# Retention and mixture of experts on one core: expert jobs of full slots dealt out between the chunks of the retention

## The chip, the cores and the metric

The kernel runs on one NeuronCore of a Trainium2 chip. The core has five engines that take their own instructions in order: PE (TensorE, matrix products), ACT (ScalarE), DVE (VectorE), POOL (GpSimd) and SP (SyncE, which here issues most of the DMA transfers). The weight loads of PE are listed apart as PEld. Times are microseconds of device time for one execution of the whole program; the metric is the median of several runs. The profile is of one further execution.

## The reference

The reference does two things, one after the other. The first is a retention: for each of 4 sequences and 8 heads, a 64 x 64 state decays by a factor per head and takes in k and v of each of 768 tokens; q times the state is the output.

```python
for t in range(S):                      # q, k, v: (4, 8, 768, 64)
    state = gamma * state + k[t] v[t]^T
    y[t] = scale * q[t] @ state
x = y.transpose(0, 2, 1, 3).reshape(3072, 512)
```

The second sends each of the 3072 rows of x to one of 8 experts:

```python
logits = x @ w_gate + modality_bias[modality_id]    # (3072, 8)
e = argmax(logits); gate = softmax(logits)[e]
out = gate * (relu(x @ w1[e]) @ w2[e])              # w1: 512 x 1024, w2: 1024 x 512
```

Which rows go to which expert is known only once the retention has run. With the inputs of the reference, 1567 rows go to expert 0, 1502 to expert 3 and 3 to expert 5; the others get none. After 6, 9, 15, 18, 21 and 24 chunks of 128 rows the counts of experts 0 and 3 are 399 and 368, 578 and 573, 979 and 940, 1187 and 1114, 1386 and 1299, 1567 and 1502.

## The kernel before

**Retention.** The 3072 tokens are worked in 24 chunks of 128, six for each sequence. `chunk(n)` (line 693) loads k and v (`load_kv`, for chunk n+2) and k and q (`load_kq`, for chunk n+3), 512 KB each, on SP's queue; POOL scales v by the decay (`decay_v`, tile vd); PE adds to the state (`state`, st), makes the scores of the next chunk (`scores`, sc), which DVE masks (tile a), turns the chunk before into token rows and logits (`tokens_out`, x; ACT copies to xs, SP stores to `x_dram`), and makes the chunk's own output from the state and from the scores (`heads_out`, y at lines 187 and 193; DVE scales it into yT). A chunk has thus a first half, st and sc, and a second half, x and y. The matrix products of this stage are in full fp32.

**Routing.** After each three chunks (a group), `route_a`, `route_b` and `scatter` (lines 239 to 303) find each token's expert and its position in the expert's list, on DVE with a few small matmuls (rk), and POOL writes token number and gate weight into a table in DRAM, `tbl`, in three indirect transfers.

**Slots and units.** The table has 96 candidates, twelve slots of 256 rows for each expert. A slot of 256 rows is one long job, a unit of 128 rows a short one. After six groups, `early_a` and `early_b` pick the two largest slots; after the last group, `final_a` and `final_b` rank all slots and write the list of the other ten slots and of what is left, in units. A register loop at the end of the kernel (`For_i` from 2 to the number of units) does units beyond the first two; with these inputs there are two units, so it runs zero times.

**Jobs.** `jobs` (line 644) is eleven slots, two units and the last slot. For each job, SP reads expert and row from the list into registers, loads the row numbers (`ids`), POOL gathers the rows from `x_dram` (xg), SP loads the expert's weights into `raw` tiles, four of 512 KB for each of the two layers, unless the expert is that of the job before (`cond=(e != old)`). ACT and DVE cut each raw piece into a high and a low part (`split_weights`, lines 462 and 464), so that three fp32r products (`PAIRS`) stand for one of fp32. PE transposes the gathered rows (`xp`), runs the first layer (line 522 for a slot, 96 matmuls of 256 columns in eight groups; 542 for a unit) and the second (line 570, 48 matmuls of 512 columns for a slot, in two halves of the rows). ACT scales the result by the gate weight and POOL scatters it to the output (line 580).

**Order.** The loop over the 24 chunks stands first. Small things are hung into it by `at(n, where, ...)`: the routing of group g into chunks 3g+4 and 3g+5; for group 5, the early list into chunks 18 and 19, registers and gathers of the first two jobs into chunk 20, the weights of the first job into chunk 21. Then `run_jobs` (line 621) goes through the jobs: a job's successor gets its registers, rows and first-layer weights at the start of the job, its first-layer cut and second-layer load between the layers, its second-layer cut at the end. The last routing and the final list are hung into the first job. This order of the program is a priority, not the last word: a planner that works with its own estimate of each instruction's time fixes each engine's order when the program is built, and takes an instruction early where its engine would stand idle and buffers are free. On the chip that order is kept, each engine strictly in order.

## Time and profile before

| | |
|---|---|
| median of 3 runs | 476.25 us (474.18 to 478.75) |
| profiled execution, its own time | 478.72 us |
| its span, first to last instruction | 476.3 us |
| mean granted PE clock | 0.951 |
| PE busy | 428.3 us, 3647 matmuls |
| DVE, ACT, POOL busy | 265.9, 209.5, 115.5 us |
| moved by q1 (SP) / by q0 (POOL) | 54.32 MB / 13.14 MB |

The page shows busy times over the whole span, and since the kernel has two stages with different limits, the views by stretch and by instruction say more than the totals. In these views, idle time before an instruction stands in brackets with what ended it. The granted clock is that of PE, 1.00 being full. The names are those of the program, with `_s` for slots and `_u` for units; `sc`, `st`, `x` and `y` belong to the retention, `xp`, `h` and `o` to the jobs.

### The profile page before, as it was taken

The page shows a single profiled execution, that of the slowest core. Times are in us where ns is not written, and L with a number is a line of the kernel's source. Part 1 is how long each engine was busy: PE and PEld are TensorE (multiplying, and loading weights), DVE is VectorE, ACT ScalarE, POOL GpSimd, SP SyncE. Part 2 cuts the span into 40 slices and gives each one's busy share as a digit, 9 for nine tenths or more (in the row PEclk, how much of TensorE's full clock was granted, in tenths as well). Part 3 has the DMA queues.
Part 4 walks back from the last instruction along what each step waited for, and adds up shares of the span by engine and source line. Part 5 has one row for each costly group of instructions (what it writes and reads, how often), then busy time and mean ns, then how long its engine had stood idle before and what let it go on. Part 6 is the DMA issues. An engine that isn't in the chain of part 4 may idle for free.

```text
span 476.3 us, 10044 instructions
## 1 busy us (share of the span) xinstructions
PE 428.3 (90%) x3647; PEld 383.6 (81%) x3647; DVE 265.9 (56%) x532; ACT 209.5 (44%) x363; POOL 115.5 (24%) x109
## 2 busy tenths in 40 slices
PE   4968989696929999999999999999999999999990
PEld 4857878585817989898989898989898989888980
DVE  2544644375508967475757574746565656588500
ACT  1211211121216546464646565656565656589400
POOL 3214343342433133231303012213030202121100
PEclk9999997898875999999999999999999999999996
DMA  8988979969658202201113562111120447577000
GB/s 290 329 272 273 247 216 270 226 190 225 208 173 335 46 23 68 67 28 64 33 58 103 170 194 67 29 61 54 38 64 26 143 153 243 187 233 308 2 24 16
DMA packets 36242, 68.53 MB, mean 144 GB/s; under 512 B 8159, under 2 KB 20703, under 8 KB 36192
## 3 DMA queue, kind: packets, MB, share of 16 engines
q1 hardware_dynamic: 30976, 54.32, 38.4%
q0 software_dynamic: 4928, 13.14, 8.1%
q8 instruction: 29, 0.48, 0.5%
q10 hardware_dynamic: 288, 0.42, 0.2%
q14 instruction: 21, 0.17, 0.2%
HBM read 92.55 MB, written 13.59 MB: 223 GB/s over the span
## 4 chain that ended last, share of the span: by engine, by line
PE 57%; issue 8%; DMA 3%; DVE 1%; POOL 1%; ACT 1%; SPq 1%; POOLq 0%; ACTq 0%
PE h_s L522 26%; PE o_s L570 26%; PE xp_s L508 2%; DMA raw<-in_w_dram 2%; DMA tbl<-rows,pos 1%; PE o_u L570 1%; PE uh_u L542 1%; POOL out_dram L580 1%; DVE lo_s L464 1%; PE x L208 0%; SPq L454 0%; PE y L187 0%; ACT hs_u L548 0%; ACT hi_u L462 0%; SPq L483 0%
## 5 line engine op out<-in xcount | busy, mean ns | idle before, releaser
L464 DVE TENSOR_TENSOR lo_s<-raw,hi_s 128x1024 fp32r<-128x1024 f32 x96 | 117.2, 1223 | 81.4 <-ACT hi_s L462 80.0
L462 ACT CAST hi_s<-raw 128x1024 fp32r<-128x1024 f32 x96 | 100.2, 1044 | 29.6 <-PE o_s L570 14.6
L522 PE MATMUL h_s<-xTh,hi_s 128*128 128x256 f32 x384 | 108.5, 283 | 0.0
L522 PE MATMUL h_s<-xTh,lo_s 128*128 128x256 f32 x384 | 108.3, 283 | 0.0
L522 PE MATMUL h_s<-xTl,hi_s 128*128 128x256 f32 x384 | 107.9, 283 | 0.1
L570 PE MATMUL o_s<-hi_s,hTh 128*128 128x512 f32 x192 | 76.2, 397 | 0.0
L570 PE MATMUL o_s<-lo_s,hTh 128*128 128x512 f32 x192 | 75.6, 394 | 0.0
L570 PE MATMUL o_s<-hi_s,hTl 128*128 128x512 f32 x192 | 75.5, 393 | 0.0
L522 PEld LDWEIGHTS h_s<-xTh,lo_s 128*128 128x128 f32 x384 | 73.6, 192 | 0.5
L522 PEld LDWEIGHTS h_s<-xTh,hi_s 128*128 128x128 f32 x384 | 73.6, 192 | 0.5
L522 PEld LDWEIGHTS h_s<-xTl,hi_s 128*128 128x128 f32 x384 | 73.2, 192 | 0.3 <-DVE xTl L478 0.3
L580 POOL DMA_INDIRECT out_dram<-o_s,ids_s x24 | 27.0, 1126 | 153.3 <-ACT o_s L579 148.5
L472 ACT ACTIVATE hTh<-h_s 128x256 fp32r<-128x256 f32 x96 | 36.8, 384 | 60.2 <-PE h_s L522 56.2
L473 DVE SCALAR_TENSOR_TENSOR hTl<-h_s,hTh 128x256 fp32r<-128x256 f32 x96 | 40.2, 420 | 27.4 <-ACT hTh L472 27.3
L212 ACT COPY xs<-x 128x272 f32<-128x272 f32 x48 | 17.4, 386 | 74.7 <-DMA x_dram<-xs 31.8
L208 PE MATMUL x<-wgt,yT 128*128 128x136 f32 x192 | 33.4, 325 | 16.7 <-DVE yT L200 16.3
L171 DVE TENSOR_TENSOR a<-sc,cst 128x512 f32<-128x512 f32 x48 | 31.0, 684 | 27.5 <-PE sc L166 23.4
L489 POOL DMA_INDIRECT xg_s<-x_dram,ids_s x24 | 29.6, 1233 | 66.6 <-PE h_s L522 29.0
L652 POOL TENSOR_TENSOR vd<-kv,cst 128x512 f32<-128x512 f32 x24 | 25.4, 1057 | 81.0 <-DMA kv<-in_qkv_dram 64.1
L208 PEld LDWEIGHTS x<-wgt,yT 128*128 128x128 f32 x192 | 28.2, 219 | 19.4 <-ACT s L233 11.0
L570 PEld LDWEIGHTS o_s<-lo_s,hTh 128*128 128x128 f32 x192 | 36.0, 188 | 8.1
L570 PEld LDWEIGHTS o_s<-hi_s,hTl 128*128 128x128 f32 x192 | 36.1, 188 | 7.8
(160 smaller groups left out, 515.3 us busy)
## 6 DMA issues: line engine op xcount, KB each, us to landing
raw<-in_w_dram SPq DMA_DIRECT2D x112, 512.0 KB
kv<-in_qkv_dram SPq DMA_DIRECT2D x24, 512.0 KB
kq<-in_qkv_dram SPq DMA_DIRECT2D x23, 512.0 KB
x_dram<-xs SPq DMA_DIRECT2D x24, 256.0 KB
dcq<-in_decq_dram SPq DMA_DIRECT2D x6, 256.0 KB
tbl<-rows,pos POOLq DMA_INDIRECT x24, 6.5
xg_s<-x_dram,ids_s POOLq DMA_INDIRECT x24, 3.9
out_dram<-o_s,ids_s POOLq DMA_INDIRECT x24, 2.8
```

Source lines behind the costliest of these rows:

```text
L171: evac[n] = nc.vector.tensor_tensor(a[:, j], pe[j].rearrange("p (h t) -> p h t", t=P), mask.unsqueeze(1).to_broadcast([P, NG, P]), op=ALU. ...
L208: nc.tensor.matmul(px[:, g], yT[:, 2 * u + g], wgt[:, 2 * u + g], start=(g == 0), stop=(g == 1), skip_group_check=True,)
L212: nc.scalar.copy(xs[:, 2 * u : 2 * u + 2], px)
L462: nc.scalar.copy(hi, raw)
L464: nc.vector.tensor_tensor(lo, raw, hi.bitcast(F32), op=ALU.subtract)
L472: nc.scalar.activation(hi, src, AF.Relu)
L473: nc.vector.scalar_tensor_tensor(lo, src, 0.0, hi.bitcast(F32), op0=ALU.max, op1=ALU.subtract)
L489: nc.gpsimd.indirect_dma_start(out=t[:, :], out_offset=None, in_=x_dram[:avail, :], in_offset=bass.IndirectOffsetOnAxis(ap=ids[:, hh, 0:1] ...
L522: nc.tensor.matmul(ph, w1c[f // 2][wi][:, o : o + P], xT[kc // 2][a][:, kc % 2, :], start=(n == 0), stop=(n == 3 * KC - 1),)
L570: nc.tensor.matmul(po, hT[f][a][:, hh * P : (hh + 1) * P], w2c[f // 2][wi][:, (f % 2) * DM : (f % 2 + 1) * DM], start=(n == 0), stop=(n == ...
L580: ins = nc.gpsimd.indirect_dma_start(out=out[:, :], out_offset=bass.IndirectOffsetOnAxis(ap=ids[:, hh, 0:1], axis=0), in_=o[:, :], in_offs ...
L652: nc.gpsimd.tensor_tensor(vds[n], vv, dec[:, n % NCH].unsqueeze(2).to_broadcast([P, H, D]), op=ALU.mult)
```

## The change

The retention is now a generator that yields after each half of a chunk, and a job is one that yields after each eighth of the first layer and after each quarter of each half of the second: 16 steps for a slot, 8 for a unit. Up to the first half of chunk 10 (`DENSE`) the retention runs alone. From there on jobs run, and after every fourth step of a job comes one half of a chunk, four halves in a slot.

For this, full slots are listed on the way: after groups 1, 2, 4, 5 and 6 (`EVENTS`), each list names two slots that are full by then and not named before. A slot that an early list does not find is replaced by an empty one (candidate 96, whose rows of the table are never written). Ties are broken by the candidate's number, upward or downward (+1 or -1), so that the last expert of a list is the first of the next. The final list has two slots and the units; the order at the end is slot, unit, slot, unit. There is room for 40 units in place of 16.

Routing is dealt out by `tick`: one entry of `todo` after each half chunk or job step. The ranking keeps one column where it had a matrix and a column, and spreads the keys with a product of ones and a diagonal. `split_weights` is now `cut`, piece by piece: the second-layer pieces are cut in the job's own first steps, the first-layer pieces of the next job in the second half of the job. A job's successor starts at its fourth step: registers, ids, gather, then first-layer weights; second-layer weights follow at the ninth step, the transposes at the thirteenth. The first job gets its registers, gather and both layers of weights at the end of chunk 7. The decay tiles `dcq` have memory of their own, vd has two buffers where it had three, and four gather buffers are set to zero in chunk 2.

```diff
-EARLY_GRP = 6
-NEARLY = 2
+
+
+EVENTS = {1: -1, 2: 1, 4: -1, 5: 1, 6: -1}
+NEV = 2
+NFIN = NSLOT - NEV * len(EVENTS)
 NTAIL = 2
-NUNIT = 16
+NUNIT = 40
+DENSE = 10
...
-    dcq = []
-    for i, tag in enumerate(("hi22", "lo22", "dcq2")):
-        dcq.append(me.tile([P, 2, NG, P], F32, tag=tag, name=f"dcq{i}"))
+    dcq = [cp.tile([P, 2, NG, P], F32, name=f"dcq{i}") for i in range(NCH // 2)]
...
+    def ranks(t, counts, which):
+        crep = passing("crep", [P, NE, SPE], BF16)
+        nc.vector.tensor_copy(crep, counts.unsqueeze(2).to_broadcast([P, NE, SPE]))
+        pc = bank(f"pc{t}")
+        nc.tensor.matmul(
+            pc[:NCAND, 0:1], crep.rearrange("p e i -> p (e i)"), ones[:, 0:1],
+            start=True, stop=True,
+        )
+        size = passing("size", [NCAND, 1])
+        nc.vector.tensor_scalar(size, pc[:NCAND, 0:1], off_c, 0.0, op0=ALU.subtract, op1=ALU.max)
+        nc.vector.tensor_scalar(
+            size, size, float(SLOT), mid["keep"], op0=ALU.min, op1=ALU.mult
+        )
+        key = passing("key", [NCAND, 1])
+        nc.vector.scalar_tensor_tensor(
+            key, size, float(P), id_c, op0=ALU.mult, op1=ALU.add if which > 0 else ALU.subtract
+        )
+        dg = passing("dg", [NCAND, NCAND])
+        nc.vector.tensor_scalar(dg, ident[:NCAND, :NCAND], key, None, op0=ALU.mult)
+        mid["rk"] = (t, size, key, dg)
+
+    def ranked():
+        t, size, key, dg = mid.pop("rk")
+        pk = bank(f"pk{t}")
+        nc.tensor.matmul(pk[:NCAND, :NCAND], lc["onef"], dg, start=True, stop=True)
+        gt = passing("gt", [NCAND, NCAND])
+        nc.vector.tensor_scalar(gt, pk[:NCAND, :NCAND], key, None, op0=ALU.is_gt)
+        rank = passing("rank", [NCAND, 1])
+        nc.vector.tensor_reduce(rank, gt, axis=AX.X, op=ALU.add)
+        return size, rank
+
+    def early(g):
+        size, rank = ranked()
+        full = passing("full", [NCAND, 1])
+        nc.vector.tensor_scalar(full, size, float(SLOT), None, op0=ALU.is_ge)
+        ohs = passing("ohs", [NCAND, NEV], BF16)
+        nc.vector.tensor_scalar(
+            ohs, lc["ord_r"][:, :NEV], rank, full, op0=ALU.is_equal, op1=ALU.mult
+        )
+        vals = lc["vals"]
+        pt = bank(f"pt{g}")
+        for i in range(2):
+            nc.tensor.matmul(
+                pt[:1, i * NEV : (i + 1) * NEV], vals[:, i : i + 1], ohs, start=True, stop=True
+            )
+        tk = passing("tk", [NCAND, 1])
+        nc.vector.tensor_reduce(tk, ohs, axis=AX.X, op=ALU.add)
+        keep = passing("keep2", [NCAND, 1])
+        nc.vector.tensor_tensor(keep, mid["keep"], tk, op=ALU.subtract)
+        mid["keep"] = keep
+        lst = lists[g] = small(f"lst{g}", [1, 2 * NEV], I32)
+        nc.vector.tensor_tensor(lst, pt[:1, : 2 * NEV], lc["base_e"], op=ALU.add)
+
...
-    def split_weights(m, tag):
-        chunks = []
-        for i, raw in enumerate(raws[m]):
-            hi = me.tile([P, QW], F32R, tag=f"hi{m}{i}", name=f"hi{m}{i}_{tag}")
-            nc.scalar.copy(hi, raw)
-            lo = me.tile([P, QW], F32R, tag=f"lo{m}{i}", name=f"lo{m}{i}_{tag}")
-            nc.vector.tensor_tensor(lo, raw, hi.bitcast(F32), op=ALU.subtract)
-            chunks.append((hi, lo))
-        return chunks
+    def cut(s, m, i):
+        hi = me.tile([P, QW], F32R, tag=f"hi{m}{i}", name=f"hi{m}{i}_{s['tag']}")
+        nc.scalar.copy(hi, raws[m][i])
+        lo = me.tile([P, QW], F32R, tag=f"lo{m}{i}", name=f"lo{m}{i}_{s['tag']}")
+        nc.vector.tensor_tensor(lo, raws[m][i], hi.bitcast(F32), op=ALU.subtract)
+        s.setdefault(f"w{m}", []).append((hi, lo))
 
...
+    def both(s):
+        yield from first_slot(s) if s["nh"] == 2 else first_unit(s)
+        yield from second(s)
+
+
+
+    def run_job(k):
+        cur = state_of[k]
+        long = cur["nh"] == 2
+        last = k + 1 == len(jobs)
+        nxt = None
+        for t, _ in enumerate(both(cur)):
+            if not long or t % 2 == 0 and t < 8:
+                i = t // 2 if long else t
+                if i < 4:
+                    cut(cur, 2, i)
+            if not last:
+                if t == (3 if long else 0):
+                    nxt = state_of[k + 1] = start_job(jobs[k + 1])
+                    raw(nxt, 1, cur)
+                if t == (8 if long else 4):
+                    raw(nxt, 2, cur)
+                if long and t in (9, 11, 13, 15):
+                    cut(nxt, 1, (t - 9) // 2)
+                if not long and t >= 4:
+                    cut(nxt, 1, t - 4)
+                if t == (12 if long else 6):
+                    flip_x(nxt)
+            yield
+
+
+    jobs = [("e", g, i) for g in EVENTS for i in range(NEV)]
+    for i in range(max(NFIN, NTAIL)):
+        jobs += [("s", 0, i)] * (i < NFIN) + [("u", 0, i)] * (i < NTAIL)
     state_of = {}
...
-        vds[n] = wk.tile([P, H, D], F32, tag="vd", name=f"vd_{n}", bufs=3)
+        vds[n] = wk.tile([P, H, D], F32, tag="vd", name=f"vd_{n}", bufs=2)
...
+    todo = []
+
+    def tick():
+        if todo:
+            todo.pop(0)()
+
+    def route(gr):
+        def b():
+            route_b(gr)
+            if gr in EVENTS or gr == NGRP - 1:
+                ranks(gr, cnt[gr + 1], EVENTS.get(gr, 1))
+
+        def c():
+            scatter(gr)
+            if gr in EVENTS:
+                early(gr)
+            elif gr == NGRP - 1:
+                final_a()
+
+        todo.append(lambda: [route_a(gr, i) for i in range(3)])
+        todo.extend([b, c])
+        if gr == NGRP - 1:
+            todo.append(final_b)
+
+    def retention():
+        prev = st = s = None
+        cur = scores(0)
+        for n in range(NN):
+            c = n % NCH
+            a, qv = cur
+            if n + 2 < NN:
+                load_kv(n + 2)
+            if n + 3 < NN:
+                load_kq(n + 3)
+            if 0 < n < NCH:
+                nc.sync.dma_start(dcq[n // 2][:, n % 2], decq[:, n])
+            if n == 1:
+                with tc.issue_after(evac[0].ins):
+                    setup()
+            if n == 2:
+                list_consts()
+
+                for i in range(4):
+                    z = me.tile([P, DM], F32, tag=f"xg{i % 2}", name=f"xgz{i}", bufs=2)
+                    nc.gpsimd.memset(z, 0.0)
+            if n + 1 < NN:
+                decay_v(n + 1)
+            vd = vds.pop(n)
+            nxt = None
+            if c + 1 < NCH:
+                if c == 0:
+                    st = bank(f"st_{n}")[:, : NG * D].rearrange("p (g e) -> p g e", g=NG)
+                nxt = state(n, st, vd)
+            if n + 1 < NN:
+                cur = scores(n + 1)
+            yield n
+            if prev is not None:
+                tokens_out(*prev)
+                if n % GRP == 0:
+                    route(n // GRP - 1)
+            yT = heads_out(n, a, vd, qv, s)
+            prev = (n, yT)
+            s = nxt
+            yield n
+        tokens_out(*prev)
+        route(NGRP - 1)
+        yield NN
+
...
-    cur = scores(0)
-    for n in range(NN):
-        chunk(n)
-    job = state_of[jobs[0]]
+    ret = retention()
+    for n in ret:
+        tick()
+        if 0 not in state_of and min(EVENTS) in lists:
+            job = state_of[0] = start_job(jobs[0])
+            raw(job, 1)
+            raw(job, 2)
+        if n == DENSE:
+            break
     flip_x(job)
-    tokens_out(*prev)
-    cut(job, 1)
-    cut(job, 2)
-
-    for i in range(3):
-        route_a(NGRP - 1, i)
-
-    def finish_a():
-        route_b(NGRP - 1)
-        scatter(NGRP - 1)
-        final_a(cnt[NGRP], lists["taken"])
-
-    run_jobs(jobs, state_of, {5: finish_a}, {0: final_b})
+    for i in range(4):
+        cut(job, 1, i)
+    for k in range(len(jobs)):
+        for t, _ in enumerate(run_job(k)):
+            tick()
+            if t % 4 == 1:
+                next(ret, None)
+    assert next(ret, None) is None and not todo
 
```

More of the change, by code (lines that the diff above doesn't have):

```diff
@@ L393, in final_a @@
[L393 to L400 removed]
+        onef = small("onef", [NCAND, NCAND])
+        nc.gpsimd.memset(onef, 1.0)
@@ L644 @@
-    jobs = [("s", i) for i in range(NSLOT - 1)]
-    jobs += [("u", i) for i in range(NTAIL)] + [("s", NSLOT - 1)]
+    def both(s):
[23 more added lines that the diff above has]
+                    flip_x(nxt)
+            yield
@@ L769 @@
         flip_x(s)
-        cut(s, 1)
-        cut(s, 2)
-        hT = first_unit("dyn", s["xT"], s["w1"], {})
-        second("dyn", 1, hT, s["w2"], s["ids"], {})
+        for m in (1, 2):
+            for i in range(4):
+                cut(s, m, i)
+        for _ in both(s):
+            pass
 def _layout(inputs):
```

328 lines of the change are left out of this document (98 added, 230 removed).

## Prediction

> **What bounds the kernel now.** I read the page first, then the busy times in four stretches, then the chain that ended last, then PE's own timeline.
>
> ```profile
> span 476.3 us, 10044 instructions
> ...
> PE 428.3 (90%) x3647; PEld 383.6 (81%) x3647; DVE 265.9 (56%) x532; ACT 209.5 (44%) x363; POOL 115.5 (24%) x109
> ```
>
> ```profile
> 0.00:62.00 62.00, 49.82 (x723) 43.34 (x723) 30.80 (x104) 12.31 (x32) 18.50 (x26) 0.97 0.93 283
> 62.00:155.60 93.60, 70.63 (x927) 60.83 (x926) 45.85 (x143) 22.83 (x53) 33.92 (x33) 0.82 0.82 227
> 155.60:464.50 308.90, 307.78 (x2002) 279.48 (x2000) 189.30 (x287) 173.69 (x279) 62.09 (x51) 1.00 0.30 96
> 464.50:476.30 11.80, 0.04 (x1) 0.00 (x0) 0.00 (x0) 0.69 (x1) 0.98 (x1) 0.61 0.04 16
> ```
>
> The columns of a stretch are its length, the busy time of PE, weight load, DVE, ACT and POOL, the granted clock, the DMA share and GB/s. PE is the engine to follow, but its 90% is an average over two different things. From 155.6 to 464.5 us the expert jobs run: PE is busy for 307.78 of 308.90 us at clock 1.00, so there is nothing to gain inside. From 62.0 to 155.6 us, the retention from chunk 10 to the end, PE is busy for 70.63 of 93.60 us, and at clock 0.82. The stretch before 62.0 stays as it is. The chain of waits shows how the jobs follow each other (start, length, what):
>
> ```profile
> 180.72 11.50 PE h_s L522 x96
> ...
> 251.09 11.50 PE h_s L522 x96
> 262.59 0.87 PE xp_s L508 x8
> 263.46 11.07 PE o_s L570 x48
> 274.53 11.50 PE h_s L522 x96
> ```
>
> A full slot costs 274.53 - 251.09 = 23.44 us and PE passes to the next one without a gap. How dense a chunk of the retention can be is on PE's timeline (start, length, line, shape; in brackets the idle time before and what ended it):
>
> ```profile
> 50.10 1.09 PE L193 MATMUL y<-a,vd 128*64 128x128 f32 x16
> ...
> 60.87 1.16 PE L166 MATMUL sc<-kq 64*128 64x128 f32 x16
> ...
> 78.98 1.16 PE L166 MATMUL sc<-kq 64*128 64x128 f32 x16
> 80.08 1.19 PE L208 MATMUL x<-wgt,yT 128*128 128x136 f32 x8
> 81.20 0.67 PE L187 MATMUL y<-kq,s 64*64 64x128 f32 x16
> 81.80 1.09 PE L193 MATMUL y<-a,vd 128*64 128x128 f32 x16
> 82.72 0.64 PE L228 MATMUL st<-vd,kv 128*64 128x64 f32 x16
> 83.28 1.16 PE L166 MATMUL sc<-kq 64*128 64x128 f32 x16
> ...
> 143.69 2.15 PE L208 MATMUL x<-wgt,yT 128*128 128x136 f32 x8 [10.30 <-DVE yT L200]
> ...
> 155.63 0.37 PE L522 MATMUL h_s<-xTh,hi_s 128*128 128x256 f32 x1
> ```
>
> From one sc to the next, 78.98 to 83.28, a chunk takes 4.30 us when nothing holds PE up: sc 1.10, x 1.12, y from the state 0.60, y from the scores 0.92, st 0.56 (differences of the starts). The group at 60.87 is the scores that chunk 10 makes for chunk 11. Between the two halves of the picture lies a pause: at 143.69 PE had waited 10.30 us, and its eight x matmuls then took 2.15 us where warm ones take 1.19.
>
> **The change, part by part.** *Dealing out.* Up to the first half of chunk 10, 61.96 us in the trace, the order of the work is nearly the old one. From there on PE gets job steps with half a chunk after every fourth of them, so the pauses of the retention have job matmuls to fill them. What is left of the retention there, packed densely: 15 x groups, 14 y from scores, 12 y from the state (chunks 12 and 18 start a sequence and have none), 10 st (chunks 17 and 23 end a sequence), 12 sc: 16.8 + 12.9 + 7.2 + 5.6 + 13.2 = 55.7 us. A half uses results made at least one half earlier: its scores, its vd and the yT that it turns into tokens were begun four job steps before, that is 4 x 11.50/8 = 5.8 us or more. That is the cover; without it a half would wait for the DVE and ACT work in front of it (below). The busy times left over: a job has, by the row below for nine jobs, 126.30/9 = 14.0 us of DVE and 13.2 of ACT, and a chunk (first stretch above, some 10.5 chunks with the setup in) at most 2.9 and 1.2; one job with two chunks is 32 us of PE, 19.8 of DVE, 15.6 of ACT. PE stays the bound.
>
> ```profile
> 180.72:391.73 211.01, 211.01 (x1371) 192.48 (x1370) 126.30 (x163) 119.25 (x181) 44.56 (x37) 1.00 0.25 79
> 252.00:264.00 12.00, 12.00 (x101) 11.88 (x100) 7.93 (x13) 7.39 (x14) 4.03 (x3) 1.00 0.51 161
> ```
>
> ```profile
> q1 hardware_dynamic: 30976, 54.32, 38.4%
> ```
>
> *Amount of work.* The reference's argmax over its own inputs sends 1567 tokens to expert 0, 1502 to expert 3 and 3 to expert 5. Counted after 6, 9, 15, 18 and 21 chunks, 2, 4, 6, 8 and 10 slots of 256 are full, so each of the five lists finds exactly its two; then two slots and two units are left. That is twelve slots and two units in both kernels: no matmul of a job is added. What is added is weights. In the old order the expert changes five times (the first 0, then 3, 0, 5, 3), 5 x 4.19 = 21.0 MB; that agrees with q1's 54.32 MB less 25.2 of k, q and v, 6.3 of x rows and about 1.9 of small loads. The new order 0 3 | 3 0 | 0 3 | 3 0 | 0 3 | 0 0 3 5 has nine, so 16.8 MB more, all but the first load spread under dense work: per 32 us about 2.1 MB of weights on average (4.2 when the expert changes), 2.6 of a chunk pair and 1.0 of gather and output, 180 to 245 GB/s where the first stretch above moved 283. The old reload around 252 us at 161 GB/s stood beside the gapless job at 251.09. I cost the later reloads at nothing; the cover is half a job between issue and first cut, 12 us.
>
> *Lists.* Four more lists and five routings come into the dense part (2, 3, 4, 5, 6); the last one was in the first job before and stays in one. In the old first job a routing with a list cost PE: job 0 starts at 155.63 on PE's timeline and its successor at 180.72 in the chain, 25.09 us against 23.44, so at most 1.65, cold matmuls included. Five cost between 0 and 8.2 us; I take 5, since the lists have short matmuls that wait for chains of DVE steps, and others can fill these waits only in part.
>
> *The first job's start.* This is the price. The first list, its gather and 4.2 MB of weights move from chunks 19 to 21 to chunk 7. The old rows say how long such a start takes (POOL's first scatter, the landing of the last one in the chain, SP's issues, ACT's first and last cast, the group of the subtractions):
>
> ```profile
> 125.14 1.01 POOL L295 DMA_INDIRECT tbl<-rows,pos  x1 [0.15 <-issue]
> ```
>
> ```profile
> 127.73 6.49 DMA tbl<-rows,pos
> ```
>
> ```profile
> 134.23 1.02 SPq L483 DMA_DIRECT2D ids_s<-tbl  x2
> ...
> 136.10 4.38 SPq L454 DMA_DIRECT2D raw<-in_w_dram  x8
> ```
>
> ```profile
> 140.79 1.04 ACT L462 CAST hi_s<-raw 128x1024 fp32r<-128x1024 f32 x1 [10.62 <-DMA raw<-in_w_dram]
> ...
> 152.52 1.05 ACT L462 CAST hi_s<-raw 128x1024 fp32r<-128x1024 f32 x1 [0.27 <-DMA raw<-in_w_dram]
> ```
>
> ```profile
> L464 DVE TENSOR_TENSOR lo_s<-raw,hi_s 128x1024 fp32r<-128x1024 f32 x96 | 117.2, 1223 | 81.4 <-ACT hi_s L462 80.0
> ```
>
> In the new order the three scatters are written behind the y of chunk 7, which ends at 51.2 (50.10 + 1.09). Three scatters take 2.59 us to the last one's issue, its landing 6.49, the weights go out 1.87 us after the ids (136.10 - 134.23), the first piece arrives 4.69 us later (140.79), and cast and subtraction take 1.04 + 1.22: from 51.5 that is 51.5 + 2.6 + 6.5 + 1.9 + 4.7 + 2.3 = 69.5; the gathered rows, their eight transposes (0.87) and the split put the first slot at about 71. SP is the engine that waits: it stands at the ids until the scatters have landed, and queued behind it are the x rows of chunk 7, the weights, and whichever k, q and v loads the planner has not put ahead. POOL stands at the gathers, with a later vd behind it. ACT and DVE can stand at the first cut of the weights, as they did for 10.62 us in the old kernel; PE's 10.30 us came of that, and I take that this comes again at the earlier place, at the cost of the same order. So PE is late by 71 - 62 = 9 us, plus 2 for cold matmuls behind the pause. The bounds: 0, if chunks 10 to 12 move up into the wait, and 25, the rival below.
>
> [...]
>
> *Sum*, against the profiled execution: 61.96 before the dense part, 9 + 2 for the start, 55.7 retention, 5 lists, 308.9 for the jobs as they ran (units included), 11.8 behind the last matmul: 454.4 us of span, 21.9 less than 476.3. That execution took 478.72 us by its own time, 2.4 more than its span, and the runs' median is 476.25. 21.9 off the median gives **454.4 us**.
>
> **The rivals.** *A costlier start.* If SP's order keeps the weights ahead of the k, q and v loads of chunk 10, these arrive only behind all eight pieces: 152.52 - 136.10 = 16.4 us instead of 4.7, then 1 MB at 283 GB/s, 3.7, then vd, st and sc, some 4: the first job begins at about 62.5 + 16.4 + 3.7 + 4 = 87, so 25 late instead of 9: 470 us. For it: the SP rows above stand in the order of the program (ids, then weights), and PE ran dry there. Against: kv loads need only a free buffer, which is there one chunk earlier. Chance 0.17.
> [...]
>
> *No loss at the start*: chunks 10 to 12 fill the wait; 454.4 - 11 = 443. Chance 0.10.
>
> *Halves that wait (slower).* PE takes its instructions in order. If ACT and DVE have a cut of weights ahead of the scores' mask or the yT that a half needs, then each of the 28 halves waits for a pair, 1.04 + 1.22 = 2.26 us: 28 x 2.26 = 63, so 518 us. It decides from (481 - 454.4)/28 = 0.95 us per half on. For it: exactly such a standing cut stopped PE at 143.69. Against: there the weights were late; with weights in time the cover of 5.8 us is more than twice the pair. Chance 0.06.
>
> *Reloads that show.* Eight later loads with two or three us of waiting each: 16 to 24 us, 470 to 478, about no change. For it: eight reloads instead of four behind the first, each with only 12 us from issue to first cut, and ids that may stand behind scatters on SP. Against: 4.69 us to the first piece. Chance 0.06.
>
> *The change does not find its slots.* An early list with a slot short runs an empty job, 23.4 us, and pays again in units: 478 or more. The counts above are exact but without any slack. Chance 0.02.
>
> **How the numbers follow.** That leaves 0.59 for the forecast, whose own range, from the bounds of lists and start, is 446 to 463. For 8 in 10 I reach from 441 (no loss at the start, lists at little) to 471 (the costlier start). One per cent is about what a measurement of this kernel can tell from no change: below 471.5 counts as faster. Faster takes the forecast, the cheap start and most of the costly one and a little of the reloads: 0.59 + 0.10 + 0.13 + 0.03 = 0.85. Same: 0.04 + 0.02 and a little of the others, 0.08. Slower: 0.07.
>
> **What would show it.** In the stretch from the first h_s matmul to the last, PE should be busy for more than 99% at clock 1.00, with slots and two chunks some 31 to 32 us apart (23.44 + 2 x 4.3 less what sequence ends save). The retention's last x should lie near 71 + 7 x 31.5 = 290 us. q1 should move about 71 MB. A pause on PE should stand between 60 and 72 us, ended by a cut's subtraction or a vd. A list's price would show as idle PE before rk, pc, pk or pt matmuls. I would be wrong if idle PE is named behind yT, the mask or a weight cut at many steps, if first h_s matmuls begin past 80 us, or if matmul counts differ from 3647 by more than the lists' few.

## The result, and the profile after

The changed kernel is slower: 492.42 us median (489.13 to 496.12, four runs) against 475.52 us (474.18 to 478.75) for the kernel before; the ratio is 1.0347, with a 95% interval from 1.0255 to 1.044. The forecast was 454.4 us with a range of 441 to 471. The profiled execution has a span of 489.4 us, 35.0 more than forecast. Single executions of one kernel differ by 1 to 3%: medians here are of all of them, ratios and intervals leave out those more than 1.5% above the fastest, and the profiles of four runs (spread routing with late weights, groups 3 to 7, later scatters, one chunk more) are of such longer executions.

The page of the changed kernel, with busy time and instructions of each engine and q1's packets, megabytes and share:

```profile
span 489.4 us, 10113 instructions
...
PE 436.2 (89%) x3669; PEld 386.2 (79%) x3669; DVE 276.5 (57%) x574; ACT 209.7 (43%) x363; POOL 122.8 (25%) x119
...
q1 hardware_dynamic: 35584, 71.07, 47.8%
```

The busy times in stretches cut at the first and the last job matmul (length, PE, weight load, DVE, ACT, POOL, granted clock, DMA share, GB/s):

```profile
0.00:91.40 91.40, 57.26 (x741) 49.44 (x741) 46.02 (x132) 20.98 (x41) 26.23 (x40) 0.86 0.85 264
91.40:477.50 386.10, 378.71 (x2929) 336.78 (x2928) 230.53 (x442) 188.00 (x321) 95.54 (x79) 0.98 0.51 158
477.50:489.40 11.90, 0.18 (x1) 0.00 (x0) 0.00 (x0) 0.69 (x1) 0.98 (x1) 0.68 0.00 1
```

q1 moved the 71 MB foreseen. The first h matmul comes at 91.4 us, where the forecast had 62 + 9 + 2 = 73: 18.4 us. From there to the last matmul it takes 386.1 us where the forecast had 55.7 + 5 + 308.9 = 369.6: 16.5 us. The end is as foreseen within 0.1. These are the 35.0.

PE's own timeline shows where it stood before the first job and inside it:

```profile
47.96 2.15 PE L210 MATMUL x<-wgt,yT 128*128 128x136 f32 x8 [7.22 <-DVE yT L202]
...
76.39 1.12 PE L230 MATMUL st<-vd,kv 128*64 128x64 f32 x16 [5.25 <-POOL vd L675]
...
86.73 0.20 PE L276 MATMUL rk<-oh,upper 128*128 128x24 bf16 x1 [7.21 <-DVE oh L259]
...
89.56 0.24 PE L358 MATMUL pc<-ones,crep 128*96 128x1 bf16 x1 [2.33 <-DVE crep L356]
...
91.43 0.58 PE L542 MATMUL h_e<-xTh,hi_e 128*128 128x256 f32 x1
...
96.19 0.19 PE L396 MATMUL pt<-ohs,vals 96*1 96x2 bf16 x2 [1.22 <-DVE ohs L390]
```

*The decay tile.* The first pause, 7.22 us near 48 us, stands where the prediction let everything be as it was. DVE's yT of chunk 5 waited for its decay tile, which SP had issued at 34.54, while POOL was sending the three scatters of group 0. DVE's line, SP's, and POOL's first scatter and the vd behind them:

```profile
47.39 0.76 DVE L202 TENSOR_TENSOR yT<-y,dcq 128x256 f32<-128x256 f32 x2 [9.16 <-DMA dcq<-in_decq_dram]
```

```profile
34.54 0.44 SPq L715 DMA_DIRECT2D dcq<-in_decq_dram  x1
```

```profile
33.17 1.15 POOL L297 DMA_INDIRECT tbl<-rows,pos  x1 [2.77 <-DVE lg L221]
...
36.90 1.06 POOL L675 TENSOR_TENSOR vd<-kv,cst 128x512 f32<-128x512 f32 x1
```

In the kernel before, the same tile was issued at 37.42 and the scatters went out at 42.62, behind a vd; DVE waited 3.36 us:

```profile
37.42 0.43 SPq L702 DMA_DIRECT2D dcq<-in_decq_dram  x1
```

```profile
42.62 1.15 POOL L295 DMA_INDIRECT tbl<-rows,pos  x1 [0.17 <-DMA kq<-in_qkv_dram]
```

```profile
44.20 0.76 DVE L200 TENSOR_TENSOR yT<-y,dcq 128x256 f32<-128x256 f32 x2 [3.36 <-DMA dcq<-in_decq_dram]
```

*The first job.* Further on, the row numbers of the first job wait for group 1's scatters, issued at 56.29 to 58.89, whose last lands 11.34 us after its issue (6.49 in the row of before). The weights go out at 70.88 and ACT casts the first piece at 74.25 (a line of the chain, and one of ACT's):

```profile
58.89 11.34 DMA tbl<-rows,pos
```

```profile
74.25 1.04 ACT L482 CAST hi_e<-raw 128x1024 fp32r<-128x1024 f32 x1 [6.48 <-DMA raw<-in_w_dram]
```

The prediction's sum has 5.8 us from the first cast to the first slot (1.04 + 1.22 for the cut, then up to 71, and 2 for cold matmuls). Here it takes 17.2. DVE's line shows the cuts of both layers, seven of 1.2 us behind one of 3.10, with the routing of group 2 in between:

```profile
75.33 3.10 DVE L484 TENSOR_TENSOR lo_e<-raw,hi_e 128x1024 fp32r<-128x1024 f32 x1 [5.61 <-ACT hi_e L482]
...
84.08 1.22 DVE L484 TENSOR_TENSOR lo_e<-raw,hi_e 128x1024 fp32r<-128x1024 f32 x1
...
85.36 1.21 DVE L484 TENSOR_TENSOR lo_e<-raw,hi_e 128x1024 fp32r<-128x1024 f32 x1
86.50 0.17 DVE L259 TENSOR_TENSOR oh<-iota3m,mn 128x24 bf16<-128x24 f32 x1
...
89.31 0.20 DVE L356 COPY crep<-cnt 128x96 bf16<-128x96 bf16 x1
89.42 1.22 DVE L484 TENSOR_TENSOR lo_e<-raw,hi_e 128x1024 fp32r<-128x1024 f32 x1
```

PE has group 2's rk and pc ahead of the transposes of the first job in its order. So it stands 7.21 and 2.33 us for oh and crep, which themselves stand behind cuts of weights, some of them second-layer weights that nobody needs yet. ACT's part of that routing, at 83.73, also stands behind a second-layer cast, which had waited 2.54 us for its piece. The 5.25 us before st at 76.39 end with a vd that POOL has behind the gathers of the first job (74.25), as the prediction said it could.

*The lists inside the jobs.* The first h matmuls of jobs 1 to 5 on PE's timeline:

```profile
128.50 0.28 PE L542 MATMUL h_e<-xTh,hi_e 128*128 128x256 f32 x1
...
161.33 0.28 PE L542 MATMUL h_e<-xTh,hi_e 128*128 128x256 f32 x1
...
194.99 0.28 PE L542 MATMUL h_e<-xTh,hi_e 128*128 128x256 f32 x1
...
228.57 0.28 PE L542 MATMUL h_e<-xTh,hi_e 128*128 128x256 f32 x1
...
265.35 0.28 PE L542 MATMUL h_e<-xTh,hi_e 128*128 128x256 f32 x1
```

A slot with two chunks takes 32.8 to 33.8 us, but the first takes 37.1 (128.50 - 91.43) and the fifth 36.8 (265.35 - 228.57). Inside the fifth:

```profile
240.70 0.38 PE L378 MATMUL pk<-dg,onef 96*96 96x96 f32 x2 [0.27 <-DVE dg L372]
242.09 0.19 PE L396 MATMUL pt<-ohs,vals 96*1 96x2 bf16 x2 [1.01 <-DVE ohs L390]
...
242.79 0.28 PE L542 MATMUL h_e<-xTh,lo_e 128*128 128x256 f32 x1
...
243.08 0.42 PE L542 MATMUL h_e<-xTh,hi_e 128*128 128x256 f32 x1
...
244.50 2.04 PE L168 MATMUL sc<-kq 64*128 64x128 f32 x16
```

pk, its DVE steps and pt are written in one entry, so pt stands on PE right behind pk and waits for DVE. The wait is 1.01 us, and then the matmuls take 0.42 in place of 0.28 and the scores 2.04 in place of 1.16: the clock is halved for some 3.5 us, with 0.95 as the mean over that slot. PE's waits from the first job matmul to the last, by what it waited for (us in total, times, longest), show lists first and hardly anything else:

```profile
PE pt L396 <- DVE ohs L390: 2.2, 2, 1.2
PE pc L358 <- DVE crep L356: 1.4, 1, 1.4
PE ut_u L577 <- ACT hs_u L565: 1.4, 2, 1.0
PE rk L276 <- DVE oh L259: 1.0, 1, 1.0
...
PE h_e L542 <- DVE yT L202: 0.3, 1, 0.3
```

### The profile page after: what moved, and what is told of

Same layout as the page of the kernel before. It is cut to its first block, busy times and chain, and to the rows that moved or that the text cites. A ratio compares the mean times of both kernels' runs of the same rounds, so it can differ in the third digit from the quotient of the medians.

```text
span 489.4 us, 10113 instructions
## 1 busy us (share of the span) xinstructions
PE 436.2 (89%) x3669; PEld 386.2 (79%) x3669; DVE 276.5 (57%) x574; ACT 209.7 (43%) x363; POOL 122.8 (25%) x119
## 3 DMA queue, kind: packets, MB, share of 16 engines
q1 hardware_dynamic: 35584, 71.07, 47.8%
## 4 chain that ended last, share of the span: by engine, by line
PE 64%; issue 8%; DMA 7%; DVE 3%; POOL 2%; ACT 1%; SPq 1%; POOLq 0%; DVEq 0%; ACTq 0%
PE h_e L542 23%; PE o_e L588 22%; DMA tbl<-rows,pos 5%; PE y L195 3%; PE x L210 3%; PE sc L168 2%; PE h_s L542 2%; PE o_s L588 2%; DMA raw<-in_w_dram 2%; PE xp_e L527 2%; DVE lo_e L484 1%; PE y L189 1%; POOL out_dram L600 1%; PE st L230 1%; PE uh_u L558 1%
## 5 line engine op out<-in xcount | busy, mean ns | idle before, releaser
L484 DVE TENSOR_TENSOR lo_e<-raw,hi_e 128x1024 fp32r<-128x1024 f32 x80 | 101.8, 1273 | 74.0 <-ACT hi_e L482 49.3
L482 ACT CAST hi_e<-raw 128x1024 fp32r<-128x1024 f32 x80 | 83.7, 1046 | 49.9 <-DMA raw<-in_w_dram 29.4
L542 PE MATMUL h_e<-xTh,hi_e 128*128 128x256 f32 x320 | 94.7, 296 | 0.3 <-DVE yT L202 0.3
L542 PE MATMUL h_e<-xTl,hi_e 128*128 128x256 f32 x320 | 92.6, 289 | 0.0
L542 PE MATMUL h_e<-xTh,lo_e 128*128 128x256 f32 x320 | 92.5, 289 | 0.0
L542 PEld LDWEIGHTS h_e<-xTh,hi_e 128*128 128x128 f32 x320 | 63.0, 197 | 2.9 <-issue 1.0
L588 PE MATMUL o_e<-hi_e,hTh 128*128 128x512 f32 x160 | 65.1, 407 | 0.0
L542 PEld LDWEIGHTS h_e<-xTh,lo_e 128*128 128x128 f32 x320 | 63.2, 197 | 0.4
L542 PEld LDWEIGHTS h_e<-xTl,hi_e 128*128 128x128 f32 x320 | 63.1, 197 | 0.2 <-DVE key L368 0.2
L588 PE MATMUL o_e<-lo_e,hTh 128*128 128x512 f32 x160 | 62.8, 392 | 0.0
L492 DVE SCALAR_TENSOR_TENSOR hTl<-h_e,hTh 128x256 fp32r<-128x256 f32 x80 | 32.8, 419 | 28.0 <-ACT hTh L491 27.9
L600 POOL DMA_INDIRECT out_dram<-o_e,ids_e x20 | 25.0, 1249 | 70.1 <-ACT o_e L599 68.2
```

The lines of the kernel that those rows point to most:

```text
L482: nc.scalar.copy(hi, raws[m][i])
L484: nc.vector.tensor_tensor(lo, raws[m][i], hi.bitcast(F32), op=ALU.subtract)
L492: nc.vector.scalar_tensor_tensor(lo, src, 0.0, hi.bitcast(F32), op0=ALU.max, op1=ALU.subtract)
L542: nc.tensor.matmul(ph, s["w1"][f // 2][wi][:, o : o + P], s["xT"][kc // 2][a][:, kc % 2, :], start=(n == 0), stop=(n == 3 * KC - 1),)
L588: nc.tensor.matmul(po, hT[f][a][:, hh * P : (hh + 1) * P], s["w2"][f // 2][wi][:, (f % 2) * DM : (f % 2 + 1) * DM], start=(n == 0), stop=( ...
L600: ins = nc.gpsimd.indirect_dma_start(out=out[:, :], out_offset=bass.IndirectOffsetOnAxis(ap=ids[:, hh, 0:1], axis=0), in_=o[:, :], in_offs ...
```

## The experiments

All runs are compared with the kernel before by the ratio of their times on the same chip; its median lay between 472.61 and 475.69 us there. "From the first h" is the time from the first job matmul to the end of the span; in the changed kernel it is 398.0 us.

### Is it the dealing out?

In the first run the retention runs alone to its end, with all else of the change; in the second three more chunks run ahead of the jobs.

```diff
-DENSE = 10
+DENSE = 24    # the second run: 13
```

> One constant differs: the retention runs to its end before the first job (24 chunks alone), so nothing is dealt out; the five lists, the early weights of the first job and the new job steps stay. Theory A (the loss sits before the first job's first matmul, where lists and 4.2 MB of weights fall into a stretch whose DMA share is 0.85 and PE stands still; the dealing itself is sound): jobs back to back at 23.4 us, PE over 99% busy in them, first slot at about 160, total 476 to 482. Theory B (halves between job steps and their lists cost more than they fill): the same total, 476 to 482, but then the changed kernel's stretch from 91 us on must be the part that is longer than retention and jobs packed. What tells apart is the next run; this one gives what the dealing as made is worth: about 10 us lost against this kernel.

> One constant differs: the dealing begins at chunk 13 instead of 10, while list, gather and weights of the first job stay at chunk 7, so chunks 10 to 12 run while the weights land. A: PE's idle time between 71 and 91 us falls from some 14 us to 4 or less, the total by about 10 us, to 480 to 484. B: only the number of halves falls, 28 to 22, and with it the excess of 16.6 us behind the start: 3 to 4 us less, 488.

Measured: 510.49 us, ratio 1.0783 (1.0721 to 1.0844), and 488.71 us, ratio 1.0354 (1.0291 to 1.0417). In the first both theories missed by 30 us. Its stretches up to and behind the first job matmul, and three of PE's pauses:

```profile
0.00:186.00 186.00, 130.88 (x1668) 112.47 (x1669) 91.99 (x298) 36.80 (x86) 52.63 (x66) 0.83 0.78 207
186.00:500.00 314.00, 309.85 (x2001) 280.57 (x2001) 186.67 (x276) 174.94 (x278) 61.33 (x52) 0.99 0.45 149
```

```profile
52.27 2.15 PE L210 MATMUL x<-wgt,yT 128*128 128x136 f32 x8 [10.60 <-DVE yT L202]
...
138.37 0.19 PE L396 MATMUL pt<-ohs,vals 96*1 96x2 bf16 x2 [4.33 <-DVE ohs L390]
...
178.36 0.19 PE L396 MATMUL pt<-ohs,vals 96*1 96x2 bf16 x2 [3.92 <-DVE ohs L390]
```

The retention alone now takes until 186.0 us, where it took until 155.6 before. So the change costs about 30 us when nothing covers it. Dealing out wins some 18 to 21 of these back (510.49 against 492.42 us, or ratio 1.0783 against 1.0347): it is not what made the kernel slower. In that stretch PE idles 20 us more and is busy 10 us more (clock 0.83 in place of 0.88). Of the idle time, waits for steps of the routing and the lists (oh, crep and ohs) grew by 18.0 us, from 1.8 to 19.8, waits behind vd by 5.0, from 6.7 to 11.7, and those for k and q fell by 3.1. The waits behind vd may come from the third vd buffer that the change took away; no run changes the buffers alone. The second run is at the changed kernel's ratio: three chunks more in front neither win nor lose.

### Routing and lists

One entry of the routing held several steps that wait for each other. Here a step's parts go into seven entries; group 1, on which the first job waits, stays as it is. Group 0 is spread as well. In the second run this is done for group 2 alone, in the third for groups 3 to 7.

```diff
-        todo.extend([b, c])
+        if gr == min(EVENTS):
+            todo.extend([b, c])
+        else:      # b1: route_b, b2: ranks, c1: scatter and ranked, c2: early or final_a
+            todo.extend([idle, b1, idle, b2, idle, c1, c2])
```

> From the second list on, routing and list are spread over seven ticks instead of three, so that the short matmuls (rk, pc, pk, pt) come at least one job step after the DVE work that they need. A: nothing in the dense part matters beside the start; within 2 us of 492. B: the list waits and the cold matmuls behind them go, 7.4 us of idle PE and as much of slow clock from 91 us on; the total falls by 5 to 12 us, 480 to 487.

> The changed kernel with the routing and list of group 2 alone dealt out over seven steps. Theory A (the spread's 16 us were two things, group 2's routing in the first job's start and the waits of the lists behind it): first h_e matmul at 84 to 88 us, 396 to 399 us from there to the end as in the changed kernel, 482 to 488 us. Theory B (all of it was group 2): 474 to 480 us.

> The changed kernel with the routing and lists of groups 3 to 7 dealt out over seven steps. Theory A: first h_e matmul at 91 to 92 us as in the changed kernel, 388 to 392 us from there to the end, 481 to 486 us. Theory B (all of it was group 2): as the changed kernel, 489 to 494 us.

Measured: all groups 476.25 us, ratio 1.0001 (0.9951 to 1.0052), more than either theory gave. Group 2 alone 487.48 us, ratio 1.0295 (1.0223 to 1.0367). Groups 3 to 7 481.77 us, ratio 1.0173 (1.0102 to 1.0243). The profiles divide it: with group 2 alone, the span of 487.0 holds 397.5 us from the first h, which comes at 89.54, as before the edit; with groups 3 to 7 the span of 485.7 holds 389.5, but the first h comes at 96.18. The first h was later there than expected because the wait for the decay tile was longer in these two profiles, 11.74 and 11.65 us on PE against 7.22:

```profile
53.44 2.15 PE L210 MATMUL x<-wgt,yT 128*128 128x136 f32 x8 [11.74 <-DVE yT L202]
```

So the lists behind the first job were worth 398.0 - 389.5 = 8.5 us. Group 2 in the first job's start was worth 91.43 - 89.54 = 1.9, or 6.4 if the 4.5 us that the decay tile was later there are put back. These are single profiles, but with all groups spread 389.5 us follow the first h as well. There the scatters of group 0 also go out later, at 36.34, and PE waits 5.14 us for the decay tile. PE's waits for rk and pc ahead of the first job are gone, and what remains there is the wait for the gathered rows:

```profile
81.01 0.66 PE L527 MATMUL xp_e<-cst,xg_e 128*128 128x128 f32 x2 [8.92 <-DMA xg_e<-x_dram,ids_e]
```

### The first job's second-layer weights

They are issued only behind the k and q of chunk 13, in the first run alone, in the second with the spread routing.

```diff
             raw(job, 1)
-            raw(job, 2)
...
     flip_x(job)
+    with tc.issue_after(kq_ins[DENSE + 3].ins):
+        raw(job, 2)
```

> The second-layer weights of the first job are issued behind the k and q of chunk 13 instead of with the first-layer weights, so 2.1 MB and four cuts leave the stretch before the first job. A: first h matmul at 82 to 86 us instead of 91.4, total down by 5 to 9 us, 483 to 487. B: no change, 490 to 493.

> The routing of groups 1 and up dealt out over seven steps instead of three, and the first job's second-layer weights issued only behind the k and q of chunk 13. Theory A (the two remedies touch different waits, routing behind PE's order and eight cuts in one run, so what they gave alone, 16 and 11 us, adds in part): first h_e matmul at 78 to 82 us, 463 to 471 us. Theory B (both remedies remove the same thing, the routing of group 2 that stood between the cuts, so the second adds nothing to the first): 474 to 478 us.

Measured: alone 481.72 us, ratio 1.0197 (1.0135 to 1.026), with the first h at 87.52; together with the spread routing 474.81 us, ratio 0.9974 (0.9921 to 1.0026), against 1.0001 without it. Alone it takes four cuts out of the way of group 2's oh, on which PE then waits 3.56 us in place of 7.21. Where group 2's routing is elsewhere already, it adds nothing that can be measured: the two remedies remove the same wait, as the second theory had it.

### The decay tile

In the first run the tile of chunk n+1 is loaded at chunk n, ahead of the loads of k, q and v. In the second no load is moved in the program, but the scatters of group 0 go three entries later and behind the vd of chunk 7. The third run is the kernel before with the first edit.

```diff
+            if n + 1 < NCH:
+                nc.sync.dma_start(dcq[(n + 1) // 2][:, (n + 1) % 2], decq[:, n + 1])
             if n + 2 < NN:
                 load_kv(n + 2)
             if n + 3 < NN:
                 load_kq(n + 3)
-            if 0 < n < NCH:
-                nc.sync.dma_start(dcq[n // 2][:, n % 2], decq[:, n])
```

```diff
-            scatter(gr)
+            with tc.issue_after(vd_ins[7 if gr == 0 else 0].ins):
+                scatter(gr)
...
-        todo.extend([b, c])
+        todo.extend([b] + [int] * 3 * (gr == 0) + [c])
```

> The changed kernel with one difference: the decay tile of chunk n+1 is loaded one chunk earlier, and ahead of that chunk's k, q and v. Theory A (the 7 us of idle PE near 48 us come of that tile's load, which stands late in a full DMA queue; time lost there is lost for good): no wait for this tile at the x of chunk 5, first h_e matmul at 82 to 85 us instead of 91.4, 481 to 485 us. Theory B (the stretch before the first job is bound by transfers as a whole, so a load that comes earlier only makes others later): the wait is gone, others of the same length stand elsewhere, first h_e matmul at 89 to 91, 489 to 493 us.

> The changed kernel, with the three scatters of group 0 moved on POOL from ahead of the vd of chunk 6 to behind the vd of chunk 7, some 10 us later; no load is moved. Theory A (the scatters, issued just as the decay tile of chunk 5 is under way, hold it up): DVE's wait for that tile falls from 9.2 us to under 4, first h_e matmul at 83 to 88 us, 482 to 488 us. Theory B (the tile is late because it stands behind k, q and v on SP, whatever the scatters do): the wait stays at 7 us or more, 489 to 495 us.

> The kernel before, with the decay tiles loaded one chunk earlier and nothing else. Theory A (that load costs the kernel before as well): its waits at x before 45 us, 6.0 us in four, go, and the time falls by 2 to 5 us, so part of what the earlier load gave is no remedy of the change. Theory B (in the kernel before the first job's late weights set the start of the jobs, so time won ahead of them is lost again): within 1 us of the kernel before.

Measured: with the earlier tile 479.7 us, ratio 1.0136 (a wide interval, 0.9873 to 1.0399); the first h comes at 80.81, 10.6 us earlier, and 397.1 us follow, as before the edit. PE's waits behind yT ahead of the first job fall from 10.0 to 1.9 us. So time lost near 48 us was lost for good. With the later scatters the median is 484.93 us (477.05 to 487.44, four runs, too far apart for a ratio). DVE's wait and the first scatter there:

```profile
43.03 0.76 DVE L202 TENSOR_TENSOR yT<-y,dcq 128x256 f32<-128x256 f32 x2 [4.45 <-DMA dcq<-in_decq_dram]
```

```profile
40.91 1.15 POOL L297 DMA_INDIRECT tbl<-rows,pos  x1 [0.17 <-DMA kq<-in_qkv_dram]
```

The wait halves, from 9.16 to 4.45, when the scatters go out 7.7 us later; with them out of the way two vd come earlier on POOL (34.77 and 39.69 in place of 36.90 and 43.36). In the kernel before, with the scatters at 42.62, DVE waits 3.36. In the changed kernel and in the three runs on routing above, where the load stands as in the change and the scatters start between 33.17 and 36.34 us, DVE waits 7.5 to 13.7. From the tile's issue to DVE's yT it takes 6.8 us in the kernel before (37.42 to 44.20), 12.9 in the changed one (34.54 to 47.39) and 10.7 with all groups spread (35.82 to 46.56). So the scatters beside the load go with the larger part of the delay; that the rest is the tile's place behind k, q and v is argued, not shown. The first h, at 88.59, missed the 83 to 88 expected and is only 2.8 us earlier. In the kernel before, the earlier tile gives 472.15 us, ratio 0.9959 (0.9917 to 1.0001): at most a little, as the weights at its first job stay late (PE waits 9.68 us there).

### All remedies, and how far they go

Spread routing, late second-layer weights and early decay tiles in one kernel, run twice; then the first-layer weights issued ahead of the row numbers; then one and two chunks more ahead of the jobs (the second-layer weights there behind the k and q of chunks 13 and 14).

> The two remedies of the run above and the earlier load of the decay tiles together. Theory A: the first h_e matmul comes 5 to 8 us earlier than without the earlier load, near 73 to 76 us; 457 to 466 us. Theory B (transfers bound the start as a whole): as the run above within 3 us.

> The kernel with spread routing, late second-layer weights and early decay tiles once more, in more rounds. Theory A (the three remedies together beat the kernel before): ratio 0.975 to 0.99 with an interval below 1. Theory B (no gain over the kernel before): the interval holds 1.

```diff
+        if first:
+            raw(s, 1)
         s["ids"], s["xg"] = gather(s["tag"], cd * unit, s["nh"], avail)
```

> As the run before, and the first job's first-layer weights are issued ahead of its row numbers, so that they don't wait for the scatters to land. Theory A (the first cut waits for the weights, which wait for the row numbers): 3 to 6 us less than the run before, 453 to 461 us. Theory B (the gathered rows, not the weights, come last at the first job): within 2 us of the run before.

```diff
-DENSE = 10
+DENSE = 11    # and 12
```

> The same with one more chunk ahead of the jobs (DENSE 11): the first transposes waited 6.0 us for gathered rows, and a dense chunk takes 4.3 us. Theory A (that wait can be filled): first h_e matmul at 75 to 77 us, 3 to 4 us less than with DENSE 10. Theory B (the added chunk's loads stand behind the first job's weights on SP, so it is late itself): first h_e matmul past 79 us, no less than with DENSE 10.

> The same with two more chunks ahead of the jobs (DENSE 12). Theory A: 8.6 us of chunks in a wait of 6.0: first h_e matmul at 78 to 80 us, 3 to 6 us less than with DENSE 10. Theory B (loads behind weights): first h_e matmul past 84 us, as DENSE 10 or slower.

Measured: all three remedies 466.66 us, ratio 0.989 (0.9723 to 1.0058), and again 466.81 us, ratio 0.9867 (0.9818 to 0.9916). By the interval of the second run, this kernel beats both the changed one and, by 1.3%, the one before. Its stretches in the second profile:

```profile
0.00:73.87 73.87, 54.80 (x736) 47.04 (x736) 35.80 (x122) 14.90 (x36) 24.50 (x39) 0.91 0.92 295
73.87:451.00 377.13, 373.33 (x2934) 332.81 (x2934) 238.38 (x453) 194.06 (x327) 96.52 (x79) 1.00 0.50 168
```

The first h comes at 73.87, close to the forecast's 73, and the jobs with their chunks take 377.1 us, 9.0 less than in the changed kernel and 7.5 more than forecast.

Weights ahead of the row numbers: 476.68 us, ratio 1.0069 (1.0017 to 1.012), 10 us worse and not 3 to 6 better. The first h comes at 82.08, some 7 to 8 us later; of the rest, 4.2 us are a wait of PE for a list's ohs. The row numbers were issued behind four weight pieces, at 64.53, and the gathers could start at 71.91, 7.4 us later. In the first run with the three remedies it was 62.32 and 64.50, 2.2 us. PE's wait for the gathered rows in this run:

```profile
79.24 0.66 PE L527 MATMUL xp_e<-cst,xg_e 128*128 128x128 f32 x2 [14.64 <-DMA xg_e<-x_dram,ids_e]
```

That is the prediction's costlier start in another pair of loads: row numbers of 2 KB, issued behind four weight pieces of 512 KB on SP, let the gathers start 7.4 us after their issue, and issued ahead of them 2.2. What makes them wait is not shown.

One chunk more in front gives 470.74 us, ratio 0.9912 (0.9865 to 0.996), first h at 78.43; two give 473.89 us, ratio 0.9986 (0.9944 to 1.0027), first h at 80.39. The wait for the gathered rows cannot be filled so: with one chunk more, PE waits 7.11 us for a yT at the same place. A third buffer for vd, as the kernel before has it, was not tried.

## Why the prediction was wrong

*What bounds the kernel, and the dense chunk.* Right in kind. In the second run with the three remedies PE is busy for 373.33 of 377.13 us at clock 1.00. The size was off: a slot with two chunks takes about 33.1 us, and one without 23.3 (357.8 to 381.1 in the changed kernel), so a dealt-out chunk with its share of routing costs 4.9 us where the prediction took 4.30. Retention and lists together, the stretch less the 308.9 us of jobs, take 68.2 us (377.1 - 308.9) in place of 55.7 + 5; in the changed kernel 77.2. (In the count of the st groups chunk 11 ends a sequence too, besides 17 and 23; the 10 is right.)

*"The stretch before 62.0 stays as it is."* This step failed first. The change moved the scatters of group 0 on POOL from 42.62 to 33.17 us, beside loads that moved 275 GB/s from 34 to 39 us, and a decay tile of 256 KB came 9 us late for DVE. Loading these tiles earlier, and nothing else, brought the first job 10.6 us earlier. The trace of the kernel before has such a wait (3.36 us), and the prediction did not look at it: it followed POOL's scatters only to the table they write, not to the loads that run beside them.

*The first job's start, 9 + 2.* Failed in three terms; with a fourth that was taken too long, they make the 18.4 us. The last scatter went out at 58.89 in place of 54.1 (51.5 + 2.6), 4.8 us late, by the step above. Its landing was taken at 6.49 us, from one row, and was 11.34; the kernel before has landings from 5.1 to 10.4. From the landing to the first cast it took 4.0 in place of 6.6 us. And from the first cast to the first slot it took 17.2 in place of 5.8, so 11.4 more: the first slot was taken to follow the first cut by 1.5 us and 2 for cold matmuls. No run shows those 2 us. In the changed kernel at clock 0.50 the eight transposes of the first job took 1.95 us where those at 259.05 take 1.03, and its first 24 h matmuls 5.75 us (3.02 from 91.43, 2.73 from 96.31) where the 24 from 265.35 take 2.87. DVE's fixed order had eight cuts there, with group 2's routing between them, and PE's had that routing ahead of the first job. The prediction named "ACT and DVE can stand at the first cut", yet did not ask which other instructions each engine had in line at that place. With the routing spread, 8.5 us remain (cast at 75.65, first h at 84.10), and PE waits there for the gathered rows, not for a cut. That the row numbers, the weights and the gathers set the start was right. But that with the remedies the first h came at 73.87 and 75.23 us, near the 73 of the sum, is in part luck, since the gathered rows came last there (waits of 5.05 and 2.42 us), which the sum has nearly at nothing.

*Lists, 5 us.* Mis-sized. The later lists alone cost 8.5 us more than when they are spread, and group 2's about 6 more in the start. The row that I took the bound from (25.09 against 23.44) had its ranking and its result in different entries, with PE busy in between; in the change they are in one entry. What came on top is the clock: in the fifth slot a wait of 1.01 us was followed by 3.5 us at clock 0.50. The prediction named the sign, idle PE before rk, pc, pk or pt, and it came.

*Cover of the halves, and the reloads.* Right. From the first job matmul on PE waits 0.3 us behind a yT in all, and no wait behind a load of weights is listed. q1's 71.07 MB are as counted.

*The rivals.* None happened as written. SP had the k, q and v of chunks 10 and 11 ahead of the weights, so it was not the costlier start (0.17), though the first job began 18.4 us late, past the 80 us named as a sign of being wrong. Nothing was won at the start, halves did not wait, and reloads did not show. The row numbers behind the weights did come late, by 7.4 in place of 2.2 us, but it took another kernel to show it. What happened had no rival: steps moved into a place where in-order engines hold other work. The chance of 0.07 for slower was far too small; an unchanged stretch and a single entry's price were assumed, not read from the order on the engines.

*What stays open.* Why, with the scatters beside it, the tile's wait still ranges from 7.5 to 13.7 us on DVE between kernels with the same loads; what two vd buffers in place of three cost; and what the rest of a chunk's 0.6 us consists of.

## What to carry to other kernels

When work is moved to an earlier stage, go through each engine's order at its new place and ask what stands behind every instruction that can wait. Small steps that wait on each other, such as matmul, vector step, matmul, belong in separate turns when an in-order engine has other work: here the spread routing took the ratio from 1.0347 to 1.0001. A run that undoes the overlap alone shows whether the overlap or its preparation costs the time: here the overlap won some 18 to 21 us, and the rest of the change lost about 30.

## What the runs showed of the hardware that was not expected

Behind small indirect scatters, the loads slowed down. After the three scatters of group 0, at 33.17 to 35.91 us, the throughput fell (the columns again are length, PE, weight load, DVE, ACT, POOL, clock, DMA share, GB/s):

```profile
34.00:39.00 5.00, 3.68 (x56) 3.21 (x58) 2.25 (x5) 0.77 (x2) 3.33 (x4) 1.00 1.09 275
39.00:42.00 3.00, 1.74 (x36) 1.48 (x32) 0.00 (x0) 0.37 (x1) 0.00 (x0) 1.00 0.64 91
```

From 275 GB/s it went to 91, while a load issued at 34.54 was still to land and three more went out from 38.62 to 40.17. In the run with earlier tiles it was 277 GB/s from 36 to 40 us and 128 from 40 to 44, behind scatters issued at 31.98 to 34.73 and with loads issued up to 39.05 and again from 41.57. A scatter's own landing took 5.1 to 10.4 us in the kernel before and 3.9 to 14.3 in the changed one. The rows have 8 bytes; no run here shows by what means the loads slow, or whether that size matters.

The clock halved behind pauses of about 1 us. In the fifth slot PE had idled for 0.27 and 1.01 us when the clock fell to 0.50 for 3.5 us. Near 330 us it fell again, behind pauses of 1.01 and 1.36 us:

```profile
332.00:335.00 3.00, 3.00 (x16) 3.00 (x16) 0.94 (x7) 0.12 (x1) 2.12 (x3) 0.50 0.26 93
```

In the second run with the three remedies it did not fall behind pauses of 1.15 and 0.64 us, at 87.31 and 89.80: the h matmuls behind the first take 0.28 us (the leading one 0.36) and the scores behind the second 1.16, where at clock 0.50, in the fifth slot above, they took 0.42 and 2.04. What decides is open.
